# A decay-attention and max-of-three-experts kernel: one expert folded through the output weights

## The chip, the cores and the metric

The kernel runs on one core of one Trainium2 chip. The metric is the time of one execution on the device, in microseconds, median of the runs. Names of engines: PE (TensorE), DVE (VectorE), ACT (ScalarE), POOL (GpSimd), SP (the queue that issues the DMAs).

## The reference, cut to what matters

```python
batch, n_heads, seq, head_dim = (8, 8, 576, 64)
n_tokens, d_model, d_ff = (4608, 512, 768)
...
    scores = scale * np.matmul(q, k.transpose(0, 1, 3, 2))
    log_f = np.log(np.clip(f, 0.0001, 1.0))
    cum = np.cumsum(log_f, axis=-1)
    decay = cum[:, :, :, None] - cum[:, :, None, :]
    causal = np.triu(np.ones((S, S), dtype=bool), k=1)
    scores = np.where(causal, -1000000000.0, scores + decay)
    scores = scores - np.max(scores, axis=-1, keepdims=True)
    attn = np.exp(scores)
    attn = attn / (np.sum(attn, axis=-1, keepdims=True) + 1e-09)
    return np.matmul(attn, v).astype(np.float32)
...
    h = np.maximum(np.maximum(x @ w1, x @ w2), x @ w3)
    return (h @ w_out).astype(np.float32)
```

x is the attention's output with the heads side by side, 4608 rows of 512. The four weight matrices come as float64.

## The kernel before

Everything is one program whose order is set by a planner. Each step is handed to `add` with its engine, a cost, the keys it reads and writes, and a priority in units of heads (head n of 64 stands near n). `Plan.emit` then runs a list schedule: on each engine it takes, of the steps that are ready by its own costs, the one with the lowest rank, and emits all steps in the order of the begin times so found. Every engine then runs its instructions strictly in that order. The planner's costs decide the order only; how long something takes is read from the trace.

The attention goes head by head: `scores` (L683: keys times queries into PSUM banks s, a maximum over keys on DVE and POOL, then a second pass and the exponential on ACT), `values` (L808 in the first batch; L841, L863 and L882 for pairs of heads, into bank t), and a normalization that leaves a [128, 576] tile U(kt) with two heads of x, transposed. Heads 0 to 7 run in float32 as 'first' heads.

The experts (MoE) run batch by batch, `moe(b)`, among the heads of later batches. Operands are split in two words, high and low (`wh`, `wl`; `xh`, `xl`; `hmh`, `hml`), and each product takes three matmuls: high-high, high-low, low-high. A batch has two chunks of its 576 rows, one of 256 and one of 320 (even batches the 256 first). `gemm1` (L1059) takes one block fb of 128 of the 768 features and one chunk: for each of three experts 4 slices of d_model by 3 words = 12 matmuls into one of three banks mp0, mp1, mp2, which `next_mp` hands out in turn. ACT copies the first expert's bank to tm (L1066), DVE takes two maxima (L1069), the last in the bank; ACT and DVE then split that bank into hmh and hml (L1072, L1074). `gemm2` (L1089) takes one block of 128 rows: 6 feature blocks by 3 words = 18 matmuls of 512 columns into a bank, a copy to `o`, and a store. Rows that straddle two batches go through `hdh`, `hdl`.

`load_weights(step)` loads unit `w{step}` (24 of them: w1, w2 and w3 by feature block as steps 3 fb + i, then w_out as 18 to 23), makes a float32 from the float64 with integer operations (L551 on ACT, L553 and L555 on DVE, through the buffers `o` and `hdl`), and splits it (L558 on ACT, L559 on DVE).

The eighth batch is done otherwise, by `last_batches`: a Strassen-Winograd scheme with 7 products in place of 8 of half size (L1230, 288 columns), whose combined weights `pair_weights` makes beforehand on DVE and ACT during heads 22 to 57 and keeps in device memory (`tdram`). Its second product is L1272 and L1381.

Of the kernel before, what the change touches and what calls it, by code (L numbers as in the profile page):

```python
# [214 lines left out]
def kernel(  # L215
# [306 lines left out]

    def load_weights(step, prio):
# [16 lines left out]
        if src.dtype == F32:  # L540
            dma(cols(raw.bitcast(F32)[:, 0:512]), src[:, :, c0:c1], w=[key], prio=DPW)
            add("DVE", 602, lambda: nc.vector.tensor_copy(x, raw[:, 0:512]), [key], [kx], prio)
        else:
# [465 lines left out]


    def pair_weights(f, i, k, tag, name, prio, btag="u4", gate=()):
        kb = [f"tb{btag}0", f"tb{btag}2"]

        def tb(q):
            return lazy(btag, [P, 4, P], F32R, "t")[:, q]

        def tl(q):
            return lazy(tag, [P, 4, P], F32R, "t")[:, q]

        e, o = 6 * f + i, 6 * f + 3 + i  # L1020
        for x, fb, n in ((0, 2 * f, e), (2, 2 * f + 1, o)):
            add("DVE", 335, lambda x=x, fb=fb: nc.vector.tensor_tensor(
                tb(slice(x, x + 2)).bitcast(F32), unit_w(i, fb)[:, 0, k::2].bitcast(F32), unit_w(i, fb)[:, 1, k::2].bitcast(F32),
                op=ALU.add), [f"wh{n}", f"wl{n}", *gate], [kb[x // 2]], prio, port=1)
        some = lambda tile_, x: (lambda: tile_(x).bitcast(F32))
        for d, a, b, r, ns in (
                (some(tl, slice(0, 3, 2)), some(tb, slice(2, 4)), some(tb, slice(0, 3, 2)), kb, 335),
                (some(tl, 1), some(tb, 3), some(tl, 0), kb[1:], 200), (some(tl, 3), some(tb, 1), some(tl, 1), kb[:1], 200)):
            add("DVE", ns, lambda d=d, a=a, b=b: nc.vector.tensor_tensor(d(), a(), b(), op=ALU.subtract), r, [name], prio, port=1)
        add("ACT", act_cost(4 * P) + 40, lambda: nc.scalar.activation(  # L1030
            tb(slice(0, 4)), tl(slice(0, 4)).bitcast(F32), AF.Copy), [name], kb, prio)
        add("DVE", dve_cost(4 * P), lambda: nc.vector.tensor_tensor(
            tl(slice(0, 4)), tl(slice(0, 4)).bitcast(F32), tb(slice(0, 4)).bitcast(F32), op=ALU.subtract), kb, [name], prio, port=1)
        for t, src, r in ((0, tb, kb), (1, tl, [name])):
            add("SP", 475, lambda t=t, src=src: nc.sync.dma_start(
                out=tdram[f, i, t][:, :, k].bitcast(F32), in_=src(slice(0, 4)).bitcast(F32)), r, [f"td{f}{i}{t}/{k}"], prio, 262144 / 360)
# [10 lines left out]
    def gemm1(b, c0, cn, fb, parts, prio):  # L1047
# [4 lines left out]
        for i in range(3):  # L1052
# [12 lines left out]
            if i == 0:  # L1065
                add("ACT", act_cost(cn), lambda m=m: nc.scalar.activation(t, m, AF.Copy), [km], [kt_], prio)  # L1066
            else:
                to, ko = (t, kt_) if i == 1 else (m, km)
                add("DVE", dve_cost(cn), lambda m=m, to=to: nc.vector.tensor_tensor(to, m, t, op=ALU.max),  # L1069
                    [km, kt_], [ko], prio)  # L1070
# [7 lines left out]
    def gemm2(hh, hl, kh, kl, col, row, prio):  # L1078

        for c0, cn in ((0, 256), (256, 256)) if row == B * S - P else ((0, DM),):  # L1080
            gemm2_part(hh, hl, kh, kl, col, row, c0, cn, prio)

    def gemm2_part(hh, hl, kh, kl, col, row, c0, cn, prio):
        mp, km = next_mp()
        cs, ds = slice(col, col + P), slice(c0, c0 + cn)
        for fb in range(FT):
            def go(fb=fb):
                for x, (l, r) in enumerate(((hh(), 0), (hh(), 1), (hl(), 0))):
                    nc.tensor.matmul(  # L1089
                        mp[:, 0:cn], l[:, fb, cs], unit_o(fb)[:, r, ds],  # L1090
                        start=fb == 0 and x == 0, stop=fb == FT - 1 and x == 2,
                    )
            add("PE", 3 * mm_cost(cn, P), go,
                [kh + str(fb), kl + str(fb), f"wh{3 * FT + fb}", f"wl{3 * FT + fb}"] + ([km] if fb else []), [km], prio)
        ko = "o" if cn == DM else f"o/{c0}"
        add("ACT", act_cost(cn), lambda: nc.scalar.activation(result()[:, ds], mp[:, 0:cn], AF.Copy), [km], [ko], prio)
        add("SP", 640, lambda: nc.sync.dma_start(out=out[row:row + P, ds], in_=result()[:, ds]),
            [ko], [f"out{row}{c0}"], prio, 512 * cn / 310)
# [4 lines left out]
    def moe(b, prio):  # L1103
# [12 lines left out]
        tot = sum(FT * 36 * mm_cost(c[1], P) + len(c[3]) * 18 * mm_cost(512, P) for c in chunks)  # L1116
        done = 0.0
        for c0, cn, parts, outs in chunks:
            for fb in range(FT):
# [1 line left out]
                done += 36 * mm_cost(cn, P)
            for hh, hl, kh, kl, col, row in outs:
                gemm2(hh, hl, kh, kl, col, base + row, prio(done / tot))
                done += 18 * mm_cost(512, P)

    def last_batches():

        M = S // 2
        OPS = ("11", "12", "22", "s1", "s2", "s3", "s4")
        AT = dict(zip(OPS, ("qs0", "qs1", "ks0", "ks1", "pf1", "ph1", "pl1")))  # L1130
        QUAD = [("tm0", 0, 0), ("tm1", 1, 0), ("mx1", 0, 1), ("gm1", 1, 1)]
        XS, YB, ZB = [(MPS[0], "mp0"), (MPS[1], "mp1")], (MPS[2], "mp2"), (TPS, "t0")
        OUT = [(SP1[0], "sp1/0"), (SP1[1], "sp1/1"), (SP1[2], "sp1/2"), (SP2, "sp2")]
        step = 3 * mm_cost(DM, P)

        def a(q, t):
            return lazy(AT[q], [P, 2, 2, M], F32R, "a")[:, t]

        def t_word(f, i, t):
            x = lazy("hl", [P, 18 * 256], F32R, "t")  # L1140
            if f == 1:
                x = lazy("xl" if t else "xh", [P, KT, S]).rearrange("p k s -> p (k s)")
                return x[:, 768 * i:768 * i + 768]
            return x[:, 768 * (2 * i + t):768 * (2 * i + t) + 768]

        def t_key(f, i, t):
            return f"T{f % 2}{i}{t}"

        def operand(f, i, p):
            e, o = unit_w(i, 2 * f), unit_w(i, 2 * f + 1)  # L1150
            if p in (6, 7, 4):
                x = {6: 0, 7: 256, 4: 512}[p]
                return lambda t, k: t_word(f, i, t)[:, x + P * k:x + P * k + P]
            tile_, k0 = {1: (e, 0), 2: (e, 2), 3: (o, 2), 5: (o, 0)}[p]
            return lambda t, k: tile_[:, t, k0 + k]

        def quad(x):
            return lazy(QUAD[x][0], [P, M], F32, "q")

        def snap(x):  # L1160
            return lazy(("pf2", "ph2", "pl2")[x], [P, M], F32, "n")

        def h_word(t, slot):
            return lazy("hml" if t else "hmh", [P, 3, 512], F32R, "t")[:, slot]

        def h_keys(slot):
            return [f"H{t}{slot}/{x}" for t in range(2) for x in range(3)]

        res = [lambda: lazy("o", [P, DM], F32, "e"), lambda: lazy("vn0", [P, DM], F32, "e")]

        def get_t(f, prio, first):
            for i in range(3):
                for t in range(2):
# [361 lines left out]
```

## Time and profile before

| | |
|---|---|
| median of 3 runs | 894.17 us (894.15 to 894.96) |
| span of the profiled execution | 892.4 us |
| what lies around the span, median less span | 1.8 us |
| PE, busy | 879.9 us, 99% |
| DVE, busy | 701.6 us, 79% |
| ACT, busy | 399.4 us, 45% |
| POOL, busy | 424.4 us, 48% |
| DMA | 144.06 MB, 161 GB/s in the mean |

The profiled execution's own time stands in the list only as its span, from the first to the last instruction; the runs' median is 1.8 us longer. Busy time is the union of an engine's instructions. Of matmuls the start is recorded and the end is modelled, so their spacing, start to start, says more than their durations. "Idle before" in a group's row is time for which the engine stood still ahead of those instructions, with what ended it.

### The profile page before, as it was taken

The page shows a single profiled execution, that of the slowest core. Times are in us where ns is not written, and L with a number is a line of the kernel's source. Part 1 is how long each engine was busy: PE and PEld are TensorE (multiplying, and loading weights), DVE is VectorE, ACT ScalarE, POOL GpSimd, SP SyncE. Part 2 cuts the span into 40 slices and gives each one's busy share as a digit, 9 for nine tenths or more (in the row PEclk, how much of TensorE's full clock was granted, in tenths as well). Part 3 has the DMA queues.
Part 4 walks back from the last instruction along what each step waited for, and adds up shares of the span by engine and source line. Part 5 has one row for each costly group of instructions (what it writes and reads, how often), then busy time and mean ns, then how long its engine had stood idle before and what let it go on. Part 6 is the DMA issues. An engine that isn't in the chain of part 4 may idle for free.

```text
span 892.4 us, 18724 instructions
## 1 busy us (share of the span) xinstructions
PE 879.9 (99%) x6574; PEld 796.3 (89%) x6574; DVE 701.6 (79%) x1572; ACT 399.4 (45%) x950; POOL 424.4 (48%) x380
## 2 busy tenths in 40 slices
PE   8999999999999999999999999999999999999998
PEld 6899988889989899989989899998988988898997
DVE  6989983778778898889989898887989888672442
ACT  6789543443334434434443443435344353342232
POOL 4543132265664546476464647556575655620000
PEclk9999999999999999999999999999999999999999
DMA  7995265665565846567576656667567565524301
GB/s 193 332 242 156 56 169 137 178 184 158 130 190 139 253 107 170 148 163 214 140 220 157 185 149 170 164 157 227 129 166 205 159 173 135 184 85 166 107 1 60
DMA packets 129263, 144.06 MB, mean 161 GB/s; under 512 B 54557, under 2 KB 88349, under 8 KB 129170
## 3 DMA queue, kind: packets, MB, share of 16 engines
q1 hardware_dynamic: 129170, 142.87, 58.8%
q8 instruction: 52, 0.85, 0.4%
q14 instruction: 41, 0.34, 0.1%
HBM read 66.73 MB, written 26.39 MB: 104 GB/s over the span
## 4 chain that ended last, share of the span: by engine, by line
PE 84%; DVE 6%; POOL 3%; issue 2%; DMA 2%; ACT 2%; SPq 1%; ACTq 0%; DVEq 0%; POOLq 0%
PE mp L1059 40%; PE mp L1089 12%; PE s L683 12%; PE mp L1230 5%; PE t L841 4%; PE t L808 2%; PE s L1272 2%; PE s L841 2%; DVE va_s L787 1%; PE t L863 1%; POOL z L795 1%; POOL gm L753 1%; DMA w<-in_moe_w_dram 1%; PE t L882 1%; PE t L1230 1%
## 5 line engine op out<-in xcount | busy, mean ns | idle before, releaser
L1059 PE MATMUL mp<-xh_r,w_r 128*128 128x320 f32 (+1 forms) x1872 | 410.2, 300 | 1.0 <-ACT tm L1066 0.3
L1059 PEld LDWEIGHTS mp<-xh_r,w_r 128*128 128x128 f32 x1872 | 310.9, 188 | 12.3 <-issue 6.1
L1059 PE MATMUL mp<-xl_r,w_r 128*128 128x320 f32 (+1 forms) x936 | 277.0, 296 | 0.0
L795 POOL PARTITION_ALL_REDUCE z<-va_s x96 | 193.4, 2021 | 153.9 <-DVE va_s L780 68.0
L753 POOL PARTITION_ALL_REDUCE gm<-mx x131 | 157.0, 1203 | 192.7 <-DVE mx L743 84.5
L1059 PEld LDWEIGHTS mp<-xl_r,w_r 128*128 128x128 f32 x936 | 176.3, 188 | 0.4
L683 PE MATMUL s<-qs_r,ks_r 128*128 128x320 f32 (+4 forms) x784 | 129.2, 284 | 2.0 <-POOL qs_r L756 1.9
L683 PEld LDWEIGHTS s<-qs_r,ks_r 128*128 128x128 f32 (+1 forms) x784 | 114.7, 181 | 10.8 <-POOL qs_r L756 4.9
L1089 PE MATMUL mp<-w_r,hmh_r 128*128 128x512 f32 x336 | 107.3, 400 | 0.3 <-ACT tm L1066 0.3
L743 DVE TENSOR_TENSOR mx<-mx,s 128x320 f32<-128x320 f32 (+3 forms) x248 | 92.1, 371 | 18.6 <-ACT mx L750 10.3
L1072 ACT ACTIVATE hmh_r<-mp 128x256 fp32r<-128x256 f32 x84 | 32.2, 383 | 90.8 <-DVE mp L1069 90.7
L1089 PEld LDWEIGHTS mp<-w_r,hmh_r 128*128 128x128 f32 x336 | 59.6, 188 | 13.5 <-issue 2.9
L572 DVE STREAM_TRANSPOSE hl<-hl 128x576 f32<-128x576 f32 x56 | 68.4, 1247 | 3.9 <-DMA hl<-in_q_dram 2.8
L1089 PE MATMUL mp<-w_r,hml_r 128*128 128x512 f32 x168 | 66.2, 394 | 0.0
L1066 ACT ACTIVATE tm<-mp 128x256 f32<-128x256 f32 (+1 forms) x84 | 34.5, 411 | 65.6 <-PE mp L1059 65.3
L771 ACT ACTIVATE pf<-s 128x512 f32<-128x512 f32 (+4 forms) x107 | 49.1, 506 | 31.2 <-PE s L683 29.0
L756 POOL CAST qs_r<-gm 1x256 fp32r<-1x256 f32 (+1 forms) x112 | 55.3, 496 | 7.0
L771 ACT ACTIVATE ph_f<-s 128x384 f32<-128x384 f32 (+2 forms) x80 | 36.0, 506 | 36.7 <-PE s L683 35.0
L712 DVE TENSOR_TENSOR s<-s,mask 128x256 f32<-128x256 f32 x96 | 40.7, 424 | 10.2 <-PE s L683 10.0
L750 ACT ACTIVATE mx<-s 128x320 f32<-128x320 f32 (+1 forms) x64 | 26.5, 417 | 49.3 <-DVE s L717 41.3
L1069 DVE TENSOR_TENSOR tm<-mp,tm 128x256 f32<-128x256 f32 (+1 forms) x84 | 37.3, 444 | 12.3 <-PE mp L1059 11.3
L1069 DVE TENSOR_TENSOR mp<-mp,tm 128x256 f32<-128x256 f32 (+1 forms) x84 | 38.8, 461 | 7.2 <-PE mp L1059 4.2
(306 smaller groups left out, 1557.3 us busy)
## 6 DMA issues: line engine op xcount, KB each, us to landing
qs_r<-hl SPq DMA_DIRECT2D x168, 144.0 KB
ks_r<-hl SPq DMA_DIRECT2D x168, 144.0 KB
w<-in_moe_w_dram SPq DMA_DIRECT2D x18, 512.0 KB
hl<-in_q_dram SPq DMA_DIRECT2D x14, 576.0 KB
hl<-in_k_dram SPq DMA_DIRECT2D x14, 576.0 KB
r_r<-rdram SPq DMA_DIRECT2D x56, 144.0 KB
out_dram<-o_r SPq DMA_DIRECT2D x31, 256.0 KB
xdram<-u SPq DMA_DIRECT2D x24, 288.0 KB
```

Of the source, the lines that this page charges most:

```text
L572: add("DVE", 1085, lambda e=e, tt=tt, xs=xs: nc.vector.transpose(tt[:, e], xs[:, e]), [key + "0"], [key + "1"], prio)
L683: nc.tensor.matmul(bank[bk][0:l.shape[-1], col:col + w], l, rhs(qa, w), start=start and bk not in begun, stop=stop, skip_group_check=True)
L743: nc.vector.tensor_tensor(mt[:, a:a + w], mt[:, a:a + w], bank[bk][:, col:col + w], op=ALU.max)
L753: add("POOL", 270 + 2.81 * nq, lambda: nc.gpsimd.partition_all_reduce(gm, mt, P, bass.bass_isa.ReduceOp.max), [km, km + "a"], [kg], prio - ...
L756: add("POOL", 110 + 0.83 * nq, lambda: nc.gpsimd.tensor_copy(QS(s)[96:97, 1, q0:q0 + nq], gm[96:97, :]), [kg], [kx], prio - (CB if n >= 12 ...
L771: add("ACT", act_cost(w), lambda bk=bk, w=w, col=col: nc.scalar.activation(px()[:, col:col + w], bank[bk][:, 0:w], AF.Exp, scale=sc), [kb[ ...
L795: add("POOL", 270 + 5.63 * nq, lambda: nc.gpsimd.partition_all_reduce(Z[:, q0:q0 + nq], blocks_sum()[:, q0:q0 + nq], P, bass.bass_isa.Redu ...
L841: nc.tensor.matmul(t[D * j:D * j + D, qa:qa + w], vn[:, j, c, 0:D], prs[j][0]()[:, col:col + w], start=x == 0, stop=True, skip_group_check ...
L1059: nc.tensor.matmul(m, unit_w(i, fb)[:, w, kt, :], xx, start=kt == 0 and x == 0, stop=kt == KT - 1 and x == 2,)
L1069: add("DVE", dve_cost(cn), lambda m=m, to=to: nc.vector.tensor_tensor(to, m, t, op=ALU.max), [km, kt_], [ko], prio)
L1089: nc.tensor.matmul(mp[:, 0:cn], l[:, fb, cs], unit_o(fb)[:, r, ds], start=fb == 0 and x == 0, stop=fb == FT - 1 and x == 2,)
L1230: nc.tensor.matmul(t[:, 0:M], w(u, k), a(q, v)[:, k], start=start and k == 0 and x == 0, stop=k == 1 and x == 2, skip_group_check=True)
```

## The change

max(x w1, x w2, x w3) = x w1 + max(0, x (w2 - w1), x (w3 - w1)). So the output is x (w1 w_out) plus the rectified maximum times w_out. The kernel after forms F = w1 w_out (512 x 512) once on the chip, and computes two experts, with difference weights, in place of three.

- `load_weights`: w1 is only made float32, in place, and not split; w2 and w3 get w1 subtracted (L602) before their split (now L604). For w1 the step returns early, so the loads of steps 12, 15, 18 and 21, which waited for the split of the step 12 before, wait for nothing.
- `turn_first(fb)`, ahead of batch 0's first `gemm1` of each block: PE turns the unit of w1 by a float32 matmul with the identity (L542, 4 of 128x128), ACT and DVE split it into w{3 fb}.
- `fold_first`, after batch 0's first chunk: F in four banks (mp0 to mp2 and the attention's t), 4 x 18 matmuls of 512 columns (L555); ACT and DVE split the four banks into units that held turned w1 (L563, L564).
- `gemm1`: experts 1 and 2 only (L1082); ACT rectifies the first (Relu, L1089), DVE takes one maximum (L1091).
- `gemm2_first`: 4 x 3 matmuls of 512 columns, x times F, into the bank that `gemm2` then goes on adding to (L1114, L1130). In a batch's second chunk two such banks are begun ahead.
- `keep_middle`: two ACT copies a batch, of the x rows that straddle two batches.
- `last_batches`, `pair_weights` and tdram are gone. Batch 7 goes through `moe` like the others, from `split_last`, which splits U directly.

```diff
+    def turn_first(fb, prio):
+        mp, km = next_mp()
...
+            for c in range(KT):
+                nc.tensor.matmul(mp[:, P * c:P * c + P], w[:, c], IDF, start=c == 0, stop=True, skip_group_check=True)
...
+        add("ACT", act_cost(DM) + 40, lambda: nc.scalar.activation(hi(), mp, AF.Copy), [km], [kh, key], prio)
+        add("DVE", dve_cost(DM), lambda: nc.vector.tensor_tensor(lo(), mp, hi().bitcast(F32), op=ALU.subtract), [km, kh, key], [kl], prio)
+
+    def fold_first(prio):
+        banks = [next_mp() for _ in range(NM)] + [(TPS, "t0")]
+        for k, (mp, km) in enumerate(banks):
+            for fb in range(FT):
+                def go(fb=fb, k=k, mp=mp):
+                    for x, (u, r) in enumerate(((0, 0), (0, 1), (1, 0))):
+                        nc.tensor.matmul(mp, unit_t(fb)[:, u, k], unit_o(fb)[:, r, :], start=fb == 0 and x == 0,
+                                         stop=fb == FT - 1 and x == 2)
...
+        for k, (mp, km) in enumerate(banks):
+            add("ACT", act_cost(DM) + 40, lambda k=k, mp=mp: nc.scalar.activation(unit_f(k)[:, 0], mp, AF.Copy), [km], [f"fw{k}0"], prio)
+            add("DVE", dve_cost(DM), lambda k=k, mp=mp: nc.vector.tensor_tensor(
+                unit_f(k)[:, 1], mp, unit_f(k)[:, 0].bitcast(F32), op=ALU.subtract), [km, f"fw{k}0"], [f"fw{k}1"], prio)
...
+        if step < 3 * FT and i == 0:
+            return
         val = cols(x.bitcast(F32))
+        if step < 3 * FT:
+            base = cols(first_word(fb))
+            add("DVE", 602, lambda: nc.vector.tensor_tensor(val, val, base, op=ALU.subtract), [kx, f"w{3 * fb}"], [kx], prio, port=1)
...
-        for i in range(3):
+        for i in (1, 2):
             mp, km = next_mp()
...
-            if i == 0:
-                add("ACT", act_cost(cn), lambda m=m: nc.scalar.activation(t, m, AF.Copy), [km], [kt_], prio)
+            if i == 1:
+                add("ACT", act_cost(cn), lambda m=m: nc.scalar.activation(t, m, AF.Relu), [km], [kt_], prio)
             else:
-                to, ko = (t, kt_) if i == 1 else (m, km)
-                add("DVE", dve_cost(cn), lambda m=m, to=to: nc.vector.tensor_tensor(to, m, t, op=ALU.max),
-                    [km, kt_], [ko], prio)
+                add("DVE", dve_cost(cn), lambda m=m: nc.vector.tensor_tensor(m, m, t, op=ALU.max),
+                    [km, kt_], [km], prio)
...
+    def gemm2_first(b, c0, col, row, prio):
...
+                for x, (u, r) in enumerate(((0, 0), (0, 1), (1, 0))):
+                    nc.tensor.matmul(mp, xs[u], unit_f(kt)[:, r], start=kt == 0 and x == 0,
+                                     stop=False, skip_group_check=True)
...
+            if c0 == 0:
+                if b == 0:
+                    fold_first(prio(done / tot))
+                keep_middle(prio(done / tot))
+            banks = []
+            ahead = 2 if c0 else 1
+            for x, (hh, hl, kh, kl, col, row) in enumerate(outs):
+                while len(banks) < min(x + ahead, len(outs)):
+                    banks.append(gemm2_first(b, c0, outs[len(banks)][4], base + outs[len(banks)][5], prio(done / tot)))
+                    done += 12 * mm_cost(512, P)
+                gemm2(banks[x], hh, hl, kh, kl, col, base + row, prio(done / tot))
...
-        if h == H - 1 and b < NOW:
+        if h == H - 1:
             at = H + K["MLAG"] + MW * b
-            get_x(b, at - K["MG"])
+            (get_x if b < B - 1 else split_last)(b, at - K["MG"])
             moe(b, lambda x, at=at: at + MW * x)
...
-    last_batches()
```

The planner places all of it anew. Where w_out is first used on PE, before (w17 is the last expert unit of the last block, w18 the first unit of w_out; pl1_xa and r are the words of x):

```order
L1059 MATMUL mp2_132<-pl1_xa_656,w17_r_1257 128x256 x2
L1059 MATMUL mp2_132<-r_93,w17_r_1257 128x256
L1059 MATMUL mp2_132<-pl1_xa_656,w17_r_1257 128x256
L1089 MATMUL mp0_130<-w18_r_1274,hmh_r_1037 128x512 x2
L1089 MATMUL mp0_130<-w18_r_1274,hml_r_1049 128x512
L683 MATMUL s2_128<-qs0_r_481,ks0_r_668 128x256
```

and after (w12 is w1's fifth unit, which is turned here; w0 is its first, turned already; w13 and w14 are difference units of the fifth block):

```order
L1082 MATMUL mp1_131<-r_93,w13_r_1028 128x256
L1082 MATMUL mp1_131<-pl1_xa_643,w13_r_1028 128x256
L542 MATMUL mp0_130<-hdl_119,w12_107 128x128 x4
L555 MATMUL t_129<-w18_r_1233,w0_r_792 128x512 x3
L1082 MATMUL mp2_132<-pl1_xa_643,w14_r_1063 128x256
L1082 MATMUL mp2_132<-u4_92,w14_r_1063 128x256
```

The first use of w_out has moved ahead of the last three expert units, into the fold's fourth bank t.

On DVE, where w18 is made and split, before:

```order
L555 SCALAR_TENSOR_TENSOR o_120<-w18_113,o_120 128x512
L559 TENSOR_TENSOR w17_r_1257<-hdl_119,w17_r_1257 128x512
L1074 TENSOR_TENSOR hml_r_1049<-mp2_132,hmh_r_1037 128x256
L1069 TENSOR_TENSOR tm1_124<-mp1_131,tm1_124 128x256
L559 TENSOR_TENSOR w18_r_1274<-o_120,w18_r_1274 128x512
```

and after (L547 splits a turned unit of w1, L604 a difference unit or one of w_out; L788 is a head's maximum):

```order
L602 TENSOR_TENSOR hdl_119<-hdl_119,w15_110 128x512
L593 TENSOR_SCALAR o_120<-w18_113 128x512
L595 SCALAR_TENSOR_TENSOR o_120<-w18_113,o_120 128x512
L547 TENSOR_TENSOR w9_r_1208<-mp0_130,w9_r_1208 128x512
L604 TENSOR_TENSOR w17_r_1211<-hdl_119,w17_r_1211 128x512
L788 TENSOR_TENSOR mx1_82<-mx1_82,s12_127 128x320
L788 TENSOR_TENSOR mx1_82<-mx1_82,s10_125 128x320
L788 TENSOR_TENSOR mx1_82<-mx1_82,s10_125 128x192
L788 TENSOR_TENSOR mx1_82<-mx1_82,s11_126 128x64
L1091 TENSOR_TENSOR mp2_132<-mp2_132,tm1_124 128x256
L604 TENSOR_TENSOR w18_r_1233<-o_120,w18_r_1233 128x512
```

Differences, splits of turned units and a head's maximum now stand ahead of w18's split.

More of the change, by code (lines that the diff above doesn't have):

```diff
@@ L539, in load_weights @@
         after = [f"wh{step - PD}"] if step >= PD else []
[L540 to L543, printed above, removed]
+        if True:
             add("SP", 560, lambda: nc.sync.dma_start(out=cols(raw), in_=src.bitcast(I32)[:, :, 2 * c0:2 * c1]),
@@ L997, in put_x, with split_last @@
         add("SP", 475, lambda: nc.sync.dma_start(out=xdram[b, kt], in_=U(i)), [f"u{i}"], [f"xd{b}{kt}"], prio, 294912 / 328)
+    def split_last(b, prio):
+        for kt in range(KT):
+            add("ACT", act_cost(S) + 50, lambda kt=kt: nc.scalar.activation(xh(kt), U(kt), AF.Copy), [f"u{kt}"], [f"xh{kt}"], prio)
+            add("DVE", dve_cost(S), lambda kt=kt: nc.vector.tensor_tensor(
+                xl(kt), U(kt), xh(kt).bitcast(F32), op=ALU.subtract), [f"u{kt}", f"xh{kt}"], [f"xl{kt}"], prio, port=1)
     def get_x(b, prio):
@@ L1008, in get_x @@
                 xl(kt), raw(), xh(kt).bitcast(F32), op=ALU.subtract), [f"xh{kt}"], [f"xl{kt}"], prio, port=1)
[L1011 to L1036, printed above, removed]
     mcount = [0]
@@ L1076, in gemm1 @@
                 [km, kh + str(fb)], [kl + str(fb)], prio)
[L1078 to L1098, printed above, removed]
@@ new lines, in gemm2, with go @@
+    def gemm2(bank, hh, hl, kh, kl, col, row, prio):
+        mp, km = bank
+        cs = slice(col, col + P)
+        last = row == B * S - P
+        for c0, cn in ((0, 256), (256, 256)) if last else ((0, DM),):
+            ds = slice(c0, c0 + cn)
+            for fb in range(FT):
+                def go(fb=fb, ds=ds):
+                    for x, (l, r) in enumerate(((hh(), 0), (hh(), 1), (hl(), 0))):
+                        nc.tensor.matmul(
+                            mp[:, ds], l[:, fb, cs], unit_o(fb)[:, r, ds],
+                            start=False, stop=fb == FT - 1 and x == 2, skip_group_check=True,
+                        )
+                kp = f"{km}/{c0}" if last else km
+                add("PE", 3 * mm_cost(cn, P), go,
+                    [kh + str(fb), kl + str(fb), f"wh{3 * FT + fb}", f"wl{3 * FT + fb}", km if fb == 0 else kp], [kp], prio)
+            ko = f"o/{c0}" if last else "o"
+            add("ACT", act_cost(cn), lambda ds=ds: nc.scalar.activation(result()[:, ds], mp[:, ds], AF.Copy), [kp], [ko], prio)
+            add("SP", 640, lambda ds=ds: nc.sync.dma_start(out=out[row:row + P, ds], in_=result()[:, ds]),
+                [ko], [f"out{row}{c0}"], prio, 512 * cn / 310)
@@ L1115, in moe, with keep_middle @@
             ]
-        tot = sum(FT * 36 * mm_cost(c[1], P) + len(c[3]) * 18 * mm_cost(512, P) for c in chunks)
+        tot = sum(FT * 24 * mm_cost(c[1], P) + len(c[3]) * 30 * mm_cost(512, P) for c in chunks)
         done = 0.0
+        odd = b % 2
+        def keep_middle(at):
+            for t in range(2):
+                add("ACT", act_cost(KT * 64), lambda t=t: nc.scalar.activation(
+                    middle()[:, t, :, 64 * odd:64 * odd + 64],
+                    lazy("xl" if t else "xh", [P, KT, S])[:, :, 0 if odd else S - 64:64 if odd else S].bitcast(F32), AF.Copy),
+                    [f"x{'hl'[t]}{kt}" for kt in range(KT)], [f"xm{t}"], at)
@@ L1118, in moe @@
         for c0, cn, parts, outs in chunks:
             for fb in range(FT):
+                if b == 0 and c0 == 0:
+                    turn_first(fb, prio(done / tot))
                 gemm1(b, c0, cn, fb, parts, prio(done / tot))
[L1121 to L1399 removed]
```

252 lines of the change are left out of this document (36 added, 216 removed).

## The prediction

> **What bounds the kernel now.** I read the busy shares first, then the chain that ended last, then the windows.
>
> ```profile
> PE 879.9 (99%) x6574; PEld 796.3 (89%) x6574; DVE 701.6 (79%) x1572; ACT 399.4 (45%) x950; POOL 424.4 (48%) x380
> PE 84%; DVE 6%; POOL 3%; issue 2%; DMA 2%; ACT 2%; SPq 1%; ACTq 0%; DVEq 0%; POOLq 0%
> ```
>
> The ends of matmuls are modelled, so 99% alone proves little. The chain says the same by other means: 84% of it is PE. The windows (PE, PEld, DVE, ACT, POOL, then clock and DMA) say how much PE waits:
>
> ```profile
> 50.00:850.00 800.00, 795.96 (x5883) 721.59 (x5882) 646.60 (x1454) 350.52 (x840) 398.00 (x335) 1.00 0.60 162
> 700.00:750.00 50.00, 48.45 (x372) 43.34 (x371) 42.56 (x92) 22.39 (x53) 28.84 (x24) 1.00 0.63 172
> ```
>
> From 50 to 850 us PE idles for 4.0 us in all, at full clock. So the kernel is as long as PE's list of work, and I price that list. A merged row of the chain holds back-to-back matmuls; its time over its count is what one costs.
>
> ```profile
> 104.73 6.06 PE mp L1059 x51
> 791.97 16.04 PE mp L1059 x108
> 808.01 7.70 PE mp L1089 x33
> 824.60 4.80 PE mp L1230 x36
> ```
>
> One matmul costs 0.119 us at 256 columns, 0.1485 at 320, 0.233 at 512 and 0.133 at 288.
>
> **PE's sum.** An expert over one chunk and one block of 128 features is 12 matmuls (4 slices of 128 by 3 word products). Dropping one of three experts in batches 0 to 6 takes 72 matmuls of 256 and 72 of 320 from each: 7 x (72 x 0.119 + 72 x 0.1485) = 134.8 us off. x times F adds 12 matmuls of 512 columns per block of 128 rows; even batches have 4 blocks, odd ones 5, so 31 in these seven: 372 x 0.233 = 86.7 us on. Batch 7 loses 378 products of 288 columns and keeps its 90 of 512; it gets 144 of 256, 144 of 320 and 60 more of 512: 17.1 + 21.4 + 14.0 - 50.3 = 2.2 us on. The fold is 72 matmuls of 512: 16.8 us. Turning w1 is 24 float32 matmuls of 128x128; the trace has eight of that kind on L918, each of which leaves two records:
>
> ```profile
> 46.34 0.61 PE L918 MATMUL mp<-hdl,rx 128*128 128x128 f32 x4
> 46.78 1.12 PE L683 MATMUL s<-ks 128*128 128x160 f32 x8
> ```
>
> Two took 0.44 us from start to start, so 24 cost 5.3 us. Sum: -134.8 + 86.7 + 2.2 + 16.8 + 5.3 = -23.8 us. All of it lies on the path, as PE idles nowhere that could hide it.
>
> **The other engines.** VectorE loses one maximum per block and chunk and all the work of pair_weights, and gets 12 differences and 10 splits:
>
> ```profile
> L1069 DVE TENSOR_TENSOR tm<-mp,tm 128x256 f32<-128x256 f32 x42 | 17.2, 410 | 1.1 <-PE mp L1059 1.0
> L1069 DVE TENSOR_TENSOR tm<-mp,tm 128x320 f32<-128x320 f32 x42 | 20.1, 478 | 11.3 <-PE mp L1059 10.4 <-ACT ph_f L771 0.6 <-ACT tm L1066 0.2
> L1022 DVE TENSOR_TENSOR u_t<-w_r 128x256 f32<-128x256 f32 x36 | 25.0, 719 | 1.2 <-DMA tdram<-u_t 1.2
> L1029 DVE TENSOR_TENSOR rx_t<-u_t,rx_t 128x128 f32<-128x128 f32 x36 | 18.2, 506 | 0.4
> L1032 DVE TENSOR_TENSOR rx_t<-rx_t,u_t 128x512 fp32r<-128x512 f32 x18 | 14.8, 821 | 4.3 <-ACT u_t L1030 4.2
> L559 DVE TENSOR_TENSOR w_r<-o,w_r x12: 673/688/924, 29.4 to 119.1; 128x512 fp32r<-128x512 f32 x12
> ```
>
> That is over 37 us of maxima and 58 us of pair_weights off, and 16 x 0.69 = 11 us on, beyond the splits of w1, which go one for one (6 off L559, 6 on with turn_first): VectorE is less of a bound than before from batch 1 on. I credit 1 us, of the 1.5 us that PE idles between 700 and 750 while pair_weights writes its last pieces; the floor is nothing, the ceiling the 4.0 us above. ScalarE swaps a copy for a rectification in the same shape and w1's six copies for those of turn_first; it gets 4 copies of F and 16 of middle rows and loses batch 7's snapshots, and at 45% busy PE covers it. Should that cover go, the middle copies hold up only a row block that is due a chunk later. The 36 stores and 36 loads through tdram leave SP's queue. Loads 12, 15 and 18 no longer wait for a split, and w18 passes the loads of two heads in that queue: those heads are scored some 40 us later, so I take nothing. Batch 7's split_last waits for batch 6's last reader of xh and for the last normalized U. Its cover is what PE still has of batch 6: today that runs alone from 791.97 to 815.7 us (rows above), while the last U is ready at 800.0. In the new order 8.4 us of gemm2 (36 x 0.233) stand between the last reader of xh and batch 7, against four splits of 1.0 us on VectorE and the copy ahead of them.
>
> ```profile
> 799.25 0.75 DVE L993 TENSOR_TENSOR u<-u,r_r 128x576 f32<-128x576 f32 x1
> L1007 DVE TENSOR_TENSOR xl_r<-xl_r,xh_r 128x576 fp32r<-128x576 f32 x24 | 23.9, 1020 | 2.7 <-ACT xh_r L1005 2.7
> 888.19 0.40 PE L1272 MATMUL s<-w_r,hml_t 128*128 128x512 f32 x1
> ```
>
> The end (last matmul at 888.19, span 892.4) stays: the last block is still copied and stored in halves.
>
> **The early stage, where a wait is added.** The fold needs all of w_out, and it stands early in PE's order. VectorE prepares the weights, and it is nearly full there:
>
> ```profile
> 60.00:70.00 10.00, 9.74 (x83) 9.41 (x83) 9.73 (x23) 9.03 (x21) 3.36 (x4) 1.00 1.03 300
> 90.00:100.00 10.00, 10.00 (x88) 10.00 (x87) 8.44 (x21) 4.96 (x13) 1.69 (x2) 1.00 0.01 3
> 110.00:120.00 10.00, 10.00 (x106) 7.86 (x106) 9.49 (x21) 5.22 (x12) 3.88 (x5) 1.00 0.61 156
> ```
>
> Today w_out's first block (the 19th split, fourth row below) is ready at 102.1 us and first used at 112.33; the last (24th) is ready at 120.6 and used at 124.33.
>
> ```profile
> 101.52 0.64 PE s L683 x5
> 112.33 0.63 PE L1089 MATMUL mp<-w_r,hmh_r 128*128 128x512 f32 x2
> 124.33 0.63 PE L1089 MATMUL mp<-w_r,hmh_r 128*128 128x512 f32 x2
> 101.45 0.67 DVE L559 TENSOR_TENSOR w_r<-o,w_r 128x512 fp32r<-128x512 f32 x1
> 119.96 0.68 DVE L559 TENSOR_TENSOR w_r<-hdl,w_r 128x512 fp32r<-128x512 f32 x1
> ```
>
> So there are 10.2 us of slack at the first use. In the new order 108 matmuls of 256 fewer (-12.8 us) and 20 float32 ones more (+4.4) stand ahead of it, and 15 score matmuls fewer (0.128 each by the first row, -1.9): PE arrives 10.3 us earlier. VectorE, up to that split, has the same heads, 12 differences and 4 turned splits more, 6 w1 splits and 3 maxima less: 10 x 0.69 - 3 x 0.41 = 5.7 us more. PE therefore waits 10.3 + 5.7 - 10.2 = 5.8 us, unless VectorE first uses up idle time, of which it has 1.6 us in the window from 90 to 100. At the last block, priced the same way, PE arrives 1.0 us earlier than now and VectorE 12 x 0.69 - 6 x 0.41 = 5.8 us later, against 3.7 us of slack: 3.1 us, inside the same wait. I take 5 us; bounds 0 (VectorE catches up) and 10 (both delays add). PE is in order, so scores of heads that are ready stand behind the waiting fold.
>
> Result: -23.8 - 1 + 5 = -19.8 us on a span of 892.4, so 872.6. The median of the runs, 894.17, is 1.8 us above that span: 874.4, say 874.5.
>
> **Rivals.** *No wait at the fold.* For it: PE never waited for a weight before. Against: the slack is used up by the counts above. Gain 23.8 us, with up to 4.0 of PE's other idle time: 866.5 to 870.5.
>
> *The fold costs more than its wait.* It holds all three MoE banks and bank t until it is copied out, so the values of heads 8 on, which need t, queue behind it, and a pause of PE may slow its clock. The rows bear on the second part:
>
> ```profile
> 1.53 3.17 PE L489 MATMUL s<-ident 128*128 128x512 bf16 x7 [1.53 <-POOL ident masks.py:199]
> 7.35 1.47 PE L489 MATMUL s<-ident 128*128 128x512 bf16 x6
> ```
>
> At the start 512 columns came every 0.42 us, 6 us later every 0.21, so PE begins at half rate for some 3 us. If the pause of 5 us brings that back, it costs half of 3 us, 1.5 us more; a blocked t holds back the values and sums of a pair of heads,
>
> ```profile
> 114.35 2.21 PE t L863 x20
> 116.56 1.34 PE t L882 x32
> ```
>
> 3.6 us of PE work that is then missing as filler; and the wait itself may reach its bound of 10. From 5 + 3.6 to 10 + 1.5 + 1: 878 to 882, and both at once 886. The Trainium skill, "TensorE: Matmul & The Clock Gate", section "HAM oscillation — how this bites in real kernels", states that an idle gap of over about 3.4 us returns the clock to half rate. By that rule my 5 us wait would count as 6.5 and the time 876; the trace has no pause that long after the start, so nothing here confirms or denies it.
>
> *The heads become the bound.* With (134.8 - 86.7) / 7 = 6.9 us less MoE work a batch, eight heads have that much less cover. VectorE's share of 646.6 in 800 us falls by the sums above, and POOL is at 398; I see a loss of 5 to 10 us at most: 880 to 885.
>
> *Slower: the banks.* Two experts over three banks: the second's bank must pass maximum, copy and difference before its next turn, two slots of 12 x 0.119 = 2.9 us later. Those steps alone are short:
>
> ```profile
> L1072 ACT ACTIVATE hmh_r<-mp 128x256 fp32r<-128x256 f32 x84 | 32.2, 383 | 90.8 <-DVE mp L1069 90.7
> L1074 DVE TENSOR_TENSOR hml_r<-mp,hmh_r 128x256 fp32r<-128x256 f32 x84 | 35.0, 416 | 7.2 <-ACT hdh_r L1072 4.9 <-ACT hmh_r L1072 1.5
> PE mp L1059 <- ACT tm L1066: 0.3, 1, 0.3
> ```
>
> 0.41 + 0.38 + 0.42 us and the hops leave over a microsecond of room, and PE waited 0.3 us for such a step in the whole run. But they queue among the heads' work. If each of the 96 blocks stalled PE by more than 20 / 96 = 0.21 us, the gain is gone; at 0.3 us each the time is 903.
>
> **Chances.** The forecast (wait of 3 to 7 us, 872 to 877) 0.57; no wait 0.17; a dearer fold 0.15; the heads 0.07; slower by the banks 0.04. The range reaches from 868 to 886 and leaves out the last and parts of the others. A measurement of this kernel tells some 0.2% from no change: faster 0.94, same 0.02, slower 0.04.
>
> **What would show it.** Right: PE's records fall from 6,574 to some 6,046 (-360 - 360 - 378 + 504 + 18 for the halved last block + 48); one idle stretch of 3 to 7 us on PE near 105 us, ended by VectorE's split of w_out; after 140 us PE idles as little as now; last values about 20 us earlier. Wrong: pauses spread over all batches (banks or heads), PE slow after the fold (clock), or no pause there at all.

## The result and the profile after

The changed kernel takes 873.95 us (median of 4 runs, 873.32 to 877.70) against 894.57 us; the ratio is 0.9771, 95% interval 0.9747 to 0.9795. The profiled execution has a span of 872.2 us at a granted clock of 0.999, 20.2 us less than before. In some of the profiled executions the first 20 us take up to 4 us longer than in others, with a granted clock of 0.74 to 0.91 there in place of 1.00, though their matmuls there are the same; so lags below are also given from behind it.

The busy shares and the engines of the chain, after:

```profile
PE 859.6 (99%) x6046; PEld 753.5 (86%) x6046; DVE 595.0 (68%) x1339; ACT 388.1 (44%) x924; POOL 418.9 (48%) x380
PE 86%; DVE 5%; POOL 2%; DMA 2%; ACT 2%; issue 1%; SPq 1%; ACTq 0%; DVEq 0%; POOLq 0%
```

PE has the 6,046 records that the sum was made for, 20.3 us less busy time, and the chain is PE as before. The long unbroken pieces of the chain give the prices of the new and the old matmuls:

```profile
102.45 0.93 PE mp L542 x8
795.16 21.12 PE mp L1082 x144
837.23 17.03 PE mp L1082 x144
854.26 5.59 PE mp L1114 x24
```

320 columns: 21.12 / 144 = 0.147 us; 256: 0.118; x times F at 512 columns: 0.233. The prediction had 0.1485, 0.119 and 0.233. A turned unit of w1 takes 0.93 us, where 0.88 was forecast.

Now the fold. VectorE's split of w18 (source `o`), and the end of the turn and the fold's first three matmuls on PE, after:

```profile
101.39 0.71 DVE L604 TENSOR_TENSOR w_r<-o,w_r 128x512 fp32r<-128x512 f32 x1
102.28 1.10 PE L542 MATMUL mp<-hdl,w 128*128 128x128 f32 x8
103.14 0.95 PE L555 MATMUL t<-w_r 128*128 128x512 f32 x3
```

PE arrives at 103.14, 9.2 us earlier than before (10.3 forecast). The split ends at 102.10, just when it ended before. PE does not wait; 1.0 us of slack is left. VectorE did its extra work earlier, in time that was idle before. Its busy time (third number behind the length) in the kernel before, then in the changed one:

```profile
20.00:60.00 40.00, 38.62 (x326) 36.29 (x325) 33.69 (x66) 32.23 (x74) 20.65 (x22) 1.00 1.01 280
60.00:100.00 40.00, 39.74 (x342) 39.41 (x342) 36.91 (x84) 31.55 (x74) 12.67 (x14) 1.00 0.51 145
```

```profile
20.00:60.00 40.00, 38.84 (x312) 35.65 (x312) 38.14 (x76) 33.28 (x76) 20.08 (x21) 1.00 1.01 297
60.00:100.00 40.00, 39.85 (x346) 39.74 (x344) 38.08 (x80) 30.98 (x72) 12.33 (x14) 1.00 0.44 134
50.00:850.00 800.00, 795.21 (x5489) 697.68 (x5488) 552.28 (x1253) 348.48 (x836) 393.46 (x337) 1.00 0.52 139
700.00:750.00 50.00, 49.25 (x336) 42.37 (x337) 36.06 (x79) 23.34 (x56) 31.06 (x25) 1.00 0.56 144
```

It is busy 5.6 us more between 20 and 100 us, in time in which it stood idle before. The last two rows, of the changed kernel, say that PE idles 4.8 us from 50 to 850 us, where it idled 4.0; from 700 to 750 it is 0.75 instead of 1.55.

So 5 us of the forecast's sum did not come, and the total still agrees. To find what took their place I lay PE's instructions of each kernel end to end at fixed prices (0.1185, 0.133, 0.1485 and 0.2335 us for the MoE's matmuls; for scores and values, which are the same in all kernels, fixed prices per column, some 230 us in all) and take how far the trace lags behind that list. "At list 20" is the matmul at which the list alone would have taken 20 us; the end is that of the last matmul:

| kernel | list, us | lag at list 20 | at 120 (behind the fold) | at the end | from 120 to the end |
|---|---|---|---|---|---|
| before | 835.5 | 12.5 | 25.9 | 52.9 | 27.0 |
| after | 812.3 | 11.9 | 26.2 | 55.9 | 29.7 |

The list is 23.2 us shorter, next to nothing (0.3 us) is lost up to the fold's end, and 2.7 us are lost behind it, spread over the batches. Together they make 20.2 us less, which is measured; the split into the three depends on the prices, by half a us or so. The waits that the profile names there, 150 to 790 us, in the changed kernel:

```profile
PE s L728 <- POOL qs_r L801: 1.7, 4, 0.7
PE mp L1082 <- ACT tm L1089: 0.7, 3, 0.4
PE mp L1082 <- DVE hml_r L1096: 0.5, 1, 0.5
```

These are only parts of them, as modelled ends of matmuls cover the rest. By start-to-start spacing, experts' matmuls come more than 0.15 us later than their price 12 times in this stretch, 4.0 us together; each time it is the first of the 12 matmuls of an expert, the one that needs a free bank. Before it was 5 times and 1.5 us, three of them at such a place. The difference, 2.5 us, is about what the table has behind the fold. The longest, in the chain of the changed kernel (start, duration):

```profile
715.90 0.42 DVE mx L785
716.32 0.34 DVE mp L1091
716.66 0.29 DVE va_s L825
716.95 0.20 DVE mp L1091
...
717.25 0.38 DVE hml_r L1096
...
717.67 1.33 PE mp L1082 x9
```

The steps that empty a bank (L1091, L1096) stand on VectorE among a head's maxima (L785) and sums (L825), and PE's next expert starts when the last is done.

### The profile page after: what moved, and what is told of

Same layout as the page of the kernel before. It is cut to its first block, busy times and chain, and to the rows that moved or that the text cites. A ratio compares the mean times of both kernels' runs of the same rounds, so it can differ in the third digit from the quotient of the medians.

```text
span 872.2 us, 17207 instructions
## 1 busy us (share of the span) xinstructions
PE 859.6 (99%) x6046; PEld 753.5 (86%) x6046; DVE 595.0 (68%) x1339; ACT 388.1 (44%) x924; POOL 418.9 (48%) x380
## 4 chain that ended last, share of the span: by engine, by line
PE 86%; DVE 5%; POOL 2%; DMA 2%; ACT 2%; issue 1%; SPq 1%; ACTq 0%; DVEq 0%; POOLq 0%
PE mp L1082 32%; PE mp L1130 15%; PE s L728 12%; PE mp L1114 11%; PE t L886 5%; PE s L886 2%; PE t L853 1%; PE mp L555 1%; PE t L908 1%; POOL gm L798 1%; POOL z L840 1%; DMA r_r<-rdram 1%; PE t L927 1%; DMA rdram<-sc 1%; DVE va_s L832 1%
## 5 line engine op out<-in xcount | busy, mean ns | idle before, releaser
L1082 PE MATMUL mp<-xh_r,w_r 128*128 128x320 f32 (+1 forms) x1440 | 314.1, 300 | 2.1 <-ACT tm L1089 0.7
L1082 PEld LDWEIGHTS mp<-xh_r,w_r 128*128 128x128 f32 x1440 | 238.5, 188 | 14.7 <-issue 5.1
L1082 PE MATMUL mp<-xl_r,w_r 128*128 128x320 f32 (+1 forms) x720 | 212.9, 296 | 0.0
L1082 PEld LDWEIGHTS mp<-xl_r,w_r 128*128 128x128 f32 x720 | 135.6, 188 | 0.5
L1130 PE MATMUL mp<-w_r,hmh_r 128*128 128x512 f32 (+1 forms) x396 | 123.0, 393 | 0.0
L788 DVE TENSOR_TENSOR mx<-mx,s 128x320 f32<-128x320 f32 (+3 forms) x248 | 92.1, 371 | 14.2 <-ACT mx L795 6.8
L1091 DVE TENSOR_TENSOR mp<-mp,tm 128x256 f32<-128x256 f32 (+1 forms) x96 | 44.6, 464 | 71.8 <-PE mp L1082 48.8
L1130 PEld LDWEIGHTS mp<-w_r,hmh_r 128*128 128x128 f32 x396 | 70.8, 188 | 15.9 <-issue 3.1
L1089 ACT ACTIVATE tm<-mp 128x256 f32<-128x256 f32 (+1 forms) x96 | 39.7, 414 | 83.5 <-PE mp L1082 83.4
L1130 PE MATMUL mp<-w_r,hml_r 128*128 128x512 f32 (+1 forms) x198 | 76.6, 387 | 0.0
L1114 PE MATMUL mp<-w_f,xh_r 128*128 128x512 f32 x240 | 76.2, 398 | 0.0
L757 DVE TENSOR_TENSOR s<-s,mask 128x256 f32<-128x256 f32 x96 | 40.6, 427 | 22.6 <-PE s L728 22.5
L1096 DVE TENSOR_TENSOR hml_r<-mp,hmh_r 128x256 fp32r<-128x256 f32 x96 | 39.8, 415 | 17.6 <-ACT hdh_r L1094 10.1
```

The costliest lines, as they stand in the source:

```text
L788: nc.vector.tensor_tensor(mt[:, a:a + w], mt[:, a:a + w], bank[bk][:, col:col + w], op=ALU.max)
L1082: nc.tensor.matmul(m, unit_w(i, fb)[:, w, kt, :], xx, start=kt == 0 and x == 0, stop=kt == KT - 1 and x == 2,)
L1091: add("DVE", dve_cost(cn), lambda m=m: nc.vector.tensor_tensor(m, m, t, op=ALU.max), [km, kt_], [km], prio)
L1114: nc.tensor.matmul(mp, xs[u], unit_f(kt)[:, r], start=kt == 0 and x == 0, stop=False, skip_group_check=True)
L1130: nc.tensor.matmul(mp[:, ds], l[:, fb, cs], unit_o(fb)[:, r, ds], start=False, stop=fb == FT - 1 and x == 2, skip_group_check=True,)
```

## The experiments

**The changed kernel again**, as the measure for the others.

> The changed kernel unchanged, as the measure for the others: 874 us, ratio 0.977 to the kernel before; both theories say the same. In its profile VectorE's split of w18 ends about 1 us ahead of its first use, and PE has no idle stretch of over 1 us after the first 20 us.

874.17 us, ratio 0.9778 (0.9753 to 0.9802); profiled span 872.2 us. The same 12 late starts of experts, 4.0 us together: these belong to the order and not to the run. PE does have one idle stretch of over 1 us, which was not expected: 1.5 us at 218.05 us, ahead of scores that wait for POOL.

**A late w_out.** The split of w18 twelve times in a row; the order of all engines stays.

```diff
-        add("DVE", 602, lambda: nc.vector.tensor_tensor(half(1), val, half(0).bitcast(F32), op=ALU.subtract),
+        add("DVE", 602, lambda: [nc.vector.tensor_tensor(half(1), val, half(0).bitcast(F32), op=ALU.subtract) for _ in range(12 if step == 3 * FT else 1)],
```

> The split of w18 (the first unit of w_out) is issued 12 times in a row, with the planner told of one; the order of every engine stays. VectorE is 11 x 0.74 = 8.1 us later with w18; PE has 1.0 us of slack there. Theory (PE's list is the bound, and PE is in order, so a wait at the fold adds in full): PE stands still for some 7 us at 103 us, and the run is 7 to 8 us longer than the changed kernel (881 to 882). Rival 1 (the clock falls back in a pause of that length): the first matmuls behind the pause come at half rate for 2 to 4 us, and the run is 8.5 to 10 us longer. Rival 2 (the wait is made good, since heads behind it are covered): under 4 us longer.

883.85 us, ratio 0.9882 (0.9857 to 0.9907), 9.7 us more than the changed kernel. The wait, PE's matmuls behind it, and windows of 2 us (PE busy first, granted clock third from the end):

```profile
PE t L555 <- DVE w_r L604: 6.7, 1, 6.7
```

```profile
111.03 1.22 PE L555 MATMUL t<-w_r 128*128 128x512 f32 x2 [6.66 <-DVE w_r L604]
112.05 0.41 PE L1082 MATMUL mp<-pl_xa,w_r 128*128 128x256 f32 x1
112.26 0.42 PE L1082 MATMUL mp<-u,w_r 128*128 128x256 f32 x1
...
115.81 0.28 PE L1082 MATMUL mp<-u,w_r 128*128 128x256 f32 x1
115.93 0.40 PE L1082 MATMUL mp<-pl_xa,w_r 128*128 128x256 f32 x2
```

```profile
108.00:110.00 2.00, 0.00 (x0) 0.00 (x0) 1.90 (x4) 0.00 (x0) 0.00 (x0) 0.68 0.00 0
112.00:114.00 2.00, 2.00 (x10) 1.95 (x9) 2.00 (x7) 0.63 (x1) 0.00 (x0) 0.50 0.00 0
116.00:118.00 2.00, 2.00 (x20) 2.00 (x20) 1.67 (x4) 0.95 (x4) 0.00 (x0) 1.00 0.37 76
```

The fold's first matmul, which takes the high word of w18 only, still starts at 103.88 us; the second, the first to read the low word that VectorE makes, waits. The wait at the fold exists as soon as VectorE is late, and it is not made good. The clock falls to 0.50 in the pause; behind it 256 columns come every 0.21 us until 115.6 us and every 0.12 thereafter, so 4.6 us at half rate cost some 2.3 us more. The lag at list 120 is 35.9 us, 9.7 above the changed kernel's: 6.7 of wait, 2.2 of clock and 0.8 from the first 20 us. The first rival is the one that was seen.

**More work for VectorE, spread.** Each difference unit split twice, and the planner told.

```diff
-        add("DVE", 602, lambda: nc.vector.tensor_tensor(half(1), val, ...),
+        add("DVE", 602 * (2 if step < 3 * FT else 1), lambda: [nc.vector.tensor_tensor(half(1), val, ...) for _ in range(2 if step < 3 * FT else 1)],
```

> Each of the 12 difference units is split twice, with the planner told of both: 12 x 0.74 = 8.9 us more work on VectorE ahead of w18's split, spread over 20 to 100 us. In the changed kernel VectorE has 3.5 us of idle time left from 20 to 100 us and PE 1.0 us of slack at w18. Theory (the predicted wait was absent because VectorE's idle time from 20 to 60 us took up the new work; that is now used up): PE waits 4 to 8 us ahead of the fold or at the difference units, and the run is 4 to 8 us longer than the changed kernel. Rival (there was never a wait to come, since the planner puts heads' work in front of the fold): under 1 us longer.

884.84 us, ratio 0.9886 (0.9857 to 0.9914), 10.7 us more. Two waits and the clock around the first:

```profile
PE mp L1082 <- DVE w_r L604: 2.4, 1, 2.4
PE t L555 <- DVE w_r L604: 1.8, 1, 1.8
```

```profile
116.00:118.00 2.00, 0.00 (x0) 0.00 (x0) 1.93 (x4) 0.00 (x0) 1.39 (x1) 1.00 0.74 153
118.00:120.00 2.00, 1.78 (x8) 1.78 (x9) 2.00 (x5) 0.15 (x1) 1.06 (x3) 0.57 0.71 181
120.00:122.00 2.00, 2.00 (x14) 2.00 (x12) 2.00 (x5) 1.93 (x5) 0.09 (x1) 0.58 0.00 0
```

The profiled span is 11.6 us longer: 3.9 of it are lost before list 20, which is not this edit's, 3.1 from there to list 80 (a wait of 1.6 us for ScalarE ahead of L963 at 64.8 us, and half rate behind it), and 6.2 between list 80 and 110, 4.2 of waits for splits and some 2 of clock; 1.5 come back behind the fold. So the theory's 4 to 8 us are there, and its rival is out.

The run bears out the theory's size, but not its account. The planner, told of the work, made another order: the fold starts at 121.96 us and not at 103.14, behind the last expert unit, and w18 is in time for it. The first wait is for a difference unit that is split twice, the second, at 139.59 us, for a late split of w_out. And VectorE idles 7.2 us from 20 to 100 us, more than the changed kernel's 3.8; so that its idle time was used up is not shown here. What the run shows is that more work on VectorE can hold PE up in this stage.

**The fold twice.**

```diff
-                    for x, (u, r) in enumerate(((0, 0), (0, 1), (1, 0))):
+                    for x, (u, r) in enumerate(2 * ((0, 0), (0, 1), (1, 0))):
...
```

> Every matmul of the fold is issued twice into its bank (72 more of 512 columns; F is twice what it should be), with the planner told of it. Theory (PE's list is the bound): 72 x 0.2335 = 16.8 us longer than the changed kernel, 16 to 17.5. Rival 1 (the fold is dearer than its matmuls, since it holds all MoE banks and bank t meanwhile): 18 to 22 us longer. Rival 2 (a longer fold covers waits of PE for VectorE): 13 to 16 us longer.

896.78 us, ratio 1.0017 (1.0005 to 1.0029), 22.6 us more. Rival 1 has the total and not the place: the list is 16.8 us longer, from list 20 to 120 the lag grows by 13.6 us (14.3 in the changed kernel), and from 120 to the end by 34.9 (29.7). List 120 lies within the doubled fold, which ends near list 134; at that end too the lag has grown as much as in the changed kernel at its fold's end, within 0.5 us. The added matmuls cost their price and no more, though the fold takes some 19 us longer; the other 5 us are lost in later batches, in another order. Late starts of experts sum to 6.0 us there.

**No Strassen for the last batch, alone**, on the kernel before.

```diff
-    NOW = B - 1
+    NOW = B
...
-            get_x(b, at - K["MG"])
+            (get_x if b < B - 1 else split_last)(b, at - K["MG"])
...
-        if n >= TG and (n - TG) % 2 == 0 and (n - TG) // 2 < 18:
+        if n >= BH:
...
-    last_batches()
```

> The kernel before with its eighth batch done as the other seven are, with three experts, and with no combined weights made beforehand: the third part of the change alone. PE's list loses 378 matmuls of 288 columns (50.3 us) and gets 216 of 256 and 216 of 320 (57.7 us), so it grows by 7.4 us. Theory (PE's list is the bound, the weights' preparation on VectorE was hidden): 7 to 8 us longer than the kernel before. Rival (VectorE's 58 us of preparation held PE up during heads 22 to 57): 3 to 6 us longer, and less idle time on PE between 300 and 800 us.

898.15 us, ratio to the kernel before 1.0042 (1.0026 to 1.0058): 4 us and not 7.5. The list is 7.5 us longer (843.0), the lag at the end 2.6 smaller. From 700 to 750 us, where PE idled 1.55 us before:

```profile
700.00:750.00 50.00, 49.85 (x386) 44.91 (x385) 39.11 (x85) 20.45 (x49) 26.88 (x23) 1.00 0.60 160
```

From list 600 to the end the lag grows by 5.1 us, before by 8.6; up to list 600 it is 0.9 us larger than before. So the rival has the size and not the place: what the Strassen scheme cost beside its matmuls was not spread over heads 22 to 57, but lay late, about the last heads and in the last batch. Whether it was the preparation of the weights or the scheme's own steps is open, as the edit takes out both.

**x F left out**, with the order kept, then with the planner told.

```diff
-                for x, (u, r) in enumerate(((0, 0), (0, 1), (1, 0))):
+                for x, (u, r) in enumerate(((0, 0), (0, 1), (1, 0))[:1 if kt == 0 else 0]):
```

> The changed kernel without x times F but for one matmul in each bank (so the output lacks most of x F); the planner is told the old cost, so the order stays. 36 x 11 = 396 matmuls of 512 columns fewer, 92.5 us. Theory (PE's list is the bound with no second bound near): 85 to 92 us shorter than the changed kernel. Rival (heads are near to being the bound: VectorE 595 us and the steps between the engines): 60 to 85 us shorter, with PE idle ahead of the scores, for POOL's maxima and VectorE.

> The run without x F again (396 matmuls of 512 columns fewer, 92.5 us, most of x F lacking in the output), but the planner is told, so the order is made for the shorter list; with the old order the run was only 15 us shorter than the changed kernel. Theory 1 (the heads' steps between PE, VectorE and POOL are the next bound, close behind PE's list): 825 to 845 us, PE idle for over 20 us ahead of the scores and its clock below 0.99. Theory 2 (only the old order was at fault, and PE's list remains the bound): 782 to 800 us, PE idle under 12 us after the first 20 us.

858.93 us (ratio 0.9595, 0.9573 to 0.9617) and 837.03 us (0.9346, 0.9310 to 0.9383): of 92.5 us of PE's work 15 and 37 us come off, the first less than even its rival's 60. The windows from 150 to 790 us of the first and the second, the first's longest wait and the second's:

```profile
150.00:790.00 640.00, 594.90 (x4026) 508.65 (x4025) 464.09 (x1067) 276.19 (x668) 365.18 (x304) 0.97 0.57 153
```

```profile
150.00:790.00 640.00, 603.04 (x4144) 523.48 (x4143) 468.93 (x1078) 279.08 (x682) 361.51 (x302) 0.99 0.58 153
```

```profile
PE s L728 <- POOL qs_r L801: 36.4, 35, 3.5
```

```profile
PE mp L1082 <- DVE hml_r L1096: 9.0, 7, 2.7
PE mp L1082 <- DVE xl_r L1058: 8.6, 9, 2.8
PE s L728 <- POOL qs_r L801: 6.8, 11, 1.4
PE mp L1082 <- DVE hdl_r L1096: 5.5, 9, 1.2
```

In the old order PE idles 45 us, 36.4 of them ahead of scores that wait for POOL's maxima: the rival named the place and not the size. In the new order no engine is full (PE 603 of 640 us, VectorE 469, POOL 362), and yet PE idles 37 us: it waits for the emptying of banks, for the words of x and for the heads' maxima. Theory 1 has the time but not the place: most of this idle time stands ahead of experts, not of scores. In the changed kernel PE's list is still the bound, but the next bound, the steps between the engines, stands close behind it: of the next 92.5 us of matmuls 60% would have been lost, at most, since the planner's numbers were not searched anew for the shorter list.

**The bank's steps first.** Rectification, maximum, copy and difference four heads earlier in priority.

```diff
-                add("ACT", act_cost(cn), lambda m=m: nc.scalar.activation(t, m, AF.Relu), [km], [kt_], prio)
+                add("ACT", act_cost(cn), lambda m=m: nc.scalar.activation(t, m, AF.Relu), [km], [kt_], prio - 4)
...
```

> In the changed kernel the four steps that empty an expert's banks (rectification, maximum, copy, difference) get a priority 4 heads earlier; nothing else. PE's list stays. Theory (the 2 us more of short waits within PE's expert matmuls, 10.0 against 7.9 us between 150 and 790 us, are waits for a bank to be emptied, queued behind heads' work): 1 to 2 us shorter than the changed kernel. Rival 1 (the waits come from elsewhere, as words of x or the switch of operands): no change within 0.7 us. Rival 2 (heads' steps now stand behind and PE waits for them): 1 to 4 us longer.

879.16 us, ratio 0.9830 (0.9813 to 0.9847), some 5 us more than the changed kernel. Late starts at a bank's first matmul fall from 12 (4.0 us) to one of 0.2 us, so the cause was named rightly. The time is lost elsewhere: from 150 to 790 us PE idles 8.0 us, where it idled 4.0 in the changed kernel, and after pauses about 615 us the granted clock is 0.50 from 620 to 622 us. In this kernel's waits stand

```profile
PE s L728 <- POOL qs_r L801: 5.0, 8, 2.2
PE mp L1082 <- DVE xl_r L1058: 2.1, 2, 1.3
```

of which the second and most of the first are new. Rival 2, in size a little beyond its 4 us. That the maxima and the split of x are late because they now queue behind the banks on VectorE fits the edit, but is not shown.

**One bank ahead.**

```diff
-            ahead = 2 if c0 else 1
+            ahead = 1
```

> In the changed kernel only one bank with x F is begun ahead of the sum with w_out, in both chunks (two in a batch's second chunk now). Theory (two of three banks taken at a chunk's end leave the experts one bank, and that is part of the short waits): 0.5 to 1.5 us shorter. Rival (the second bank covers the wait for the last rectified block's words): 1 to 4 us longer, up to 8 chunks of 0.5 us.

881.98 us, ratio 0.9869 (0.9848 to 0.9891), some 8 us more. The rival has the sign, at twice its largest size: from list 120 to the end the lag grows by 37.3 us, matmuls of experts that come over 0.15 us late sum to 7.7 us, and the two longest of these waits are for words of x:

```profile
PE mp L1082 <- DVE xl_r L1058: 2.8, 2, 1.4
PE mp L1082 <- ACT tm L1089: 1.4, 4, 0.6
```

That is not the wait it named, for the last rectified block; why this order splits x late is open.

**Another order.** Two sets of the planner's numbers, found apart; of the first:

```diff
-    LEAD, MLAG, WP, WR = 2.661, -0.1, -1.003, 0.566
+    LEAD, MLAG, WP, WR = 2.912, -0.1, -1.003, 0.566
-    UP, VO, FO, XO = 0.291, 1.296, -0.366, -4.973
+    UP, VO, FO, XO = 0.244, 1.296, -0.366, -4.973
...
-... AF.Relu), [km], [kt_], prio)
+... AF.Relu), [km], [kt_], prio + -0.628)
```

> The changed kernel with eight numbers of the planner moved (heads 0.25 earlier, the rectification 0.63 and the last difference 0.21 of a head earlier, thresholds by hundredths), so that in the planner's own account PE waits less; the work is the same. Theory (the 2.5 us of waits for a bank and 2 us for POOL's maxima between 150 and 790 us come from an order made for another list, and another order avoids them): 868 to 872 us, with waits of over 0.15 us in the experts' stream down from 4.0 to under 2 us. Rival (the order is as good as it gets, what is left are switches between streams, which no order of this kind avoids): 873 to 877 us.

> As the run before with another set of numbers, found independently (batches 8.17 heads apart, the first expert copy 0.15 of a head earlier, heads 0.16 earlier): theory 868 to 872 us, rival 873 to 877 us. If one of the two sets gains and the other loses, the gain is that of single orders and not of a rule.

871.61 us (ratio 0.9735, 0.9711 to 0.9758) and 868.33 us (0.9699, 0.9679 to 0.9720). The first interval overlaps the changed kernel's (0.9747 to 0.9795), so that gain of some 2 us is not clear of noise by itself; the second is. The list is the same. In both profiles no start of an expert is later than its price by 0.15 us between 150 and 790 us, and PE idles less there (before the bracket, of 640 us: 636.03 in the changed kernel):

```profile
150.00:790.00 640.00, 637.61 (x4344) 555.65 (x4345) 462.39 (x1062) 275.05 (x668) 361.24 (x300) 1.00 0.58 152
```

```profile
150.00:790.00 640.00, 638.51 (x4342) 557.46 (x4341) 462.52 (x1062) 274.67 (x666) 364.44 (x302) 1.00 0.57 152
```

From list 120 to the end the lag grows by 24.4 and 23.0 us, against 29.7. That is more than the 4.0 us of late starts, so these orders also save time elsewhere; where is open.

**The kernel before in another order**, found in the same way.

> The kernel before with its planner's numbers moved in the same way as in the two runs of the changed kernel that gained 3 and 6 us (heads' loads 0.48 of a head earlier, normalization 0.21 later, four more by little): the best set for its own list that a search of the same kind in the planner's account found. There it gains 2.0 us; the changed kernel gained 7.6. Theory (before and changed kernel have the same numbers, and these fit the list of the kernel before; the changed kernel lost by them): 891 to 895 us, within 0.3% of the kernel before. Rival (any of the two gains as much by new numbers, so the bank waits aren't the change's): 887 to 890 us, ratio 0.993 to 0.996.

896.18 us against 896.07, ratio 1.0008 (0.9991 to 1.0024): nothing. In its trace 8 experts start late, by 4.3 us together, where the kernel before had 5 and 1.5 us, so the planner's account of PE's waits is not the chip's. The planner's numbers are the same in both kernels. That they fit the list of the kernel before, and that the changed kernel's late starts are the price of an order made with numbers of another list, agrees with these three runs; one set for the kernel before can't show that no better one exists.

## Why the prediction was right, and where it was not

- *PE's list is the bound.* Right. It was priced at -23.8 us; the count of matmuls is as forecast, the prices are nearly so, and the list is 23.2 us shorter.
- *The wait of 5 us at the fold.* Wrong: 0. PE came nearly as early as forecast (9.2 us, 10.3 forecast), and VectorE's 5.7 us of new work are there (5.6 us more busy time). The step that failed is "unless VectorE first uses up idle time, of which it has 1.6 us in the window from 90 to 100": the windows from 20 to 100 us show 9.4 us of idle time before, 6.3 of it from 20 to 60, a stretch that the prediction has no row of. 5.6 of the 9.4 us were filled, and the split of w18 ended when it did before. The late w_out shows that the mechanism is real and was 1.0 us away.
- *Relief of 1 us.* Too small at one end and more than taken back at the other. Without Strassen the lag falls by 2.6 us; in the changed kernel it rises by 2.7 behind the fold, as 12 experts start late. The bank rival named this mechanism, with 0.21 us for each of 96 blocks as the point of no gain; 12 late starts of 0.34 us are a fifth of that.
- *The sum.* Forecast: -23.8 - 1 + 5 = -19.8. Measured: -23.2 + 0.3 + 2.7 = -20.2. The total agrees since a wait that did not come (5 us) is nearly made up by others: 2.7 us lost behind the fold, where the sum has 1 us of relief and nothing for late starts, 0.3 us before it, and a list that is 0.6 us longer than priced. The 872 to 877 us belonged to a wait of 3 to 7 us at the fold; the time fell there without it. The cause behind the number is the list; the rest of the working was luck.
- *What would show it.* Number of PE's records: right. The idle stretch near 105 us: absent. PE idle after 140 us as now: nearly. The last normalized U is ready at 783.6 us, 16.5 us earlier (forecast: last values about 20 us earlier). The experts' unbroken run behind the last values begins at 773.92, before at 791.97, 18.0 us earlier.

```profile
782.80 0.75 DVE L1038 TENSOR_TENSOR u<-u,r_r 128x576 f32<-128x576 f32 x1
```

```profile
773.92 7.24 PE mp L1082 x48
```

- *Rivals.* No wait at the fold happened, but its 866.5 to 870.5 us needed the rest unchanged; another order then gave 868.3. A dearer fold: the doubled fold speaks against its banks, and the clock part is real once PE does pause. The heads as the bound: not here; with x F left out they, the banks and x are.

## What to carry to other kernels

Where an engine is to take on more work ahead of a deadline, sum its idle time over the whole stretch from its first input to that deadline, not in a window at the end. After a change of the bounding engine's list, have the planner's numbers searched anew: here the better of two sets was worth another 0.7% on the changed kernel, and one set nothing on the old one. A shorter list pays in full only until the steps between engines take over; leaving out a piece of it shows how far away that is.

## What the hardware showed

A pause of PE can cost more than its length: 6.7 us (late w_out) were followed by 4.6 us at half rate, and a pause of 2.4 us (spread work) by a clock of 0.57 and 0.58 in the next two windows of 2 us. The Trainium skill, "TensorE: Matmul & The Clock Gate", section "HAM oscillation — how this bites in real kernels", tells of gaps over about 3.4 us; the longer pause agrees, the shorter shows that less can do. The length alone does not decide: in the second run without x F a pause of 2.8 us at 393.7 us left the clock at 1.00, while in the run with spread work one of 1.6 us at 64.8 us was followed by 0.50 from 68 to 70 us. What decides between them is open here.
